# Opening of a fused attention and two feed-forward blocks on one core: a constant's operation that loads the exp table, weight loads and narrowings set behind the first head pairs, and more zero products on TensorE

## The chip, the core and the metric

The kernel runs on one core of one Trainium2 chip. The metric is device time in microseconds (us), the median of the runs. Engine names are those of the profile: PE is TensorE (PEld its weight loads), DVE VectorE, ACT ScalarE, POOL GpSimd, SP SyncE, whose queue issues every DMA here.

## The reference, cut to what matters

Causal attention (2 batches, 12 heads, 448 rows, head size 64) feeds two feed-forward blocks in a row.

```python
scores = scale * np.matmul(q, k.transpose(0, 1, 3, 2))
scores = np.where(np.triu(np.ones((seq, seq), bool), k=1), -1e9, scores)
attn = np.exp(scores - scores.max(-1, keepdims=True))
x = attn / (attn.sum(-1, keepdims=True) + 1e-9) @ v      # 896 tokens x 768
h = x @ w_in                                             # 768 -> 2048
x = np.where(h >= 1, h, np.where(h <= -1, 0, (h + 1) ** 2 / 4)) @ w_out
g = x @ w_gate; out = (g * sigmoid(g) * (x @ w_val)) @ moe2_w_out
```

## The kernel before

**Attention.** The work goes by pairs of heads. Rows 0 to 223 of each batch are token group 0: twelve pairs, one step each, here steps 0 to 11. Rows 224 to 447 are group 1: again twelve pairs, two steps each (336 and 448 key columns), steps 12 to 35. A step is a chain: `scores` on PE (L245, then the mask added by a product with `mask_b`, L251), `greatest` on DVE (row maxima L263, scaled and negated L265), `exps` on ACT (L277), `normalize` on DVE (L288, L289, L301), `turn` on PE (transposes, L312), `turned` on ACT (copy out, L321), `values` on PE (L332, L345), `x_hi` on ACT and `x_lo` on DVE (L352, L356). The tile `s` has two buffers, so the scores of step k+1 wait until the exps of step k-1 have been read out.

**Weights.** Every weight tile (128 x 768, 64-bit words) goes through four DVE or POOL operations and one on ACT (`Weights.operations`): L106, L111 and L115 narrow it to 32 bits, L123 (ACT) and L124 split it into `wh` and `wl`. The first nine tiles are prepared on DVE while the attention runs, a few operations a step (`W.tick`, `TICKS`). The load of a tile is issued from SP; `wraw` has two buffers.

**Products that fill.** From step 14 on, products of the first feed-forward block (`filler`, L68 to L70, here fill products) stand between the attention's PE work. Before that, `zeros` issues products of a zeroed tile (128x512 bf16, L366) into the bank `warm`: 18 (`WARM`) at the start and `HOLD` of them in each of steps 0 to 13. `warm` and the first fill product use the same PSUM buffer, so that product comes after the last zero product.

**Order.** The program's order above is only a priority: a list scheduler in the framework settles the order of each engine's queue when the kernel is built, from its own estimate of when an operand is ready. Each engine then runs its queue strictly in that order. The zero products depend on nothing and go wherever the scheduler sees PE free. `tc.keep_in_program_order(x)` holds `x` at its written place in its engine's queue.

Of the kernel before, what the change touches and what calls it, by code (L numbers as in the profile page):

```python
# [8 lines left out]
F32 = mybir.dt.float32  # L9
# [3 lines left out]
AF = mybir.ActivationFunctionType  # L13
# [14 lines left out]
HALF = DM // 2  # L28
WB = 768
WARM = 18  # L30
HOLD = 1
AHEAD = 3
LASTB = 2
WBUFS = 4
# [13 lines left out]
TURN1 = "A"  # L48
NORM0 = "V"
NORM1 = "V"  # L50
TICKS = (1, 0, 3)


@with_exitstack
def fused_kernel(ctx: ExitStack, tc: tile.TileContext, qk, v, w_in, w_out, w_gv, w_o2, out):
    nc = tc.nc

    const = ctx.enter_context(tc.tile_pool(name="const", bufs=1))
    ident = const.tile([128, 128], F32, name="ident")
    ident_b = const.tile([128, C], BF16, name="ident_b")  # L60
    mask_b = const.tile([128, C], BF16, name="mask_b")
    half_b = const.tile([128, 1], F32, name="half_b")
    xy = ctx.enter_context(tc.tile_pool(name="xy", bufs=2))
    wp = ctx.enter_context(tc.tile_pool(name="wp", bufs=WBUFS))
    ev = ctx.enter_context(tc.tile_pool(name="ev", bufs=2))
# [11 lines left out]
    class Weights:  # L77
# [8 lines left out]
        def load(self, upto):  # L86
            while self.loaded < min(upto, len(self.srcs)):
                src, n = self.srcs[self.loaded]
                t = wp.tile([128, WB], I64, tag="raw", name="wraw", bufs=2)
                nc.sync.dma_start(out=t[:, :n], in_=src)  # L90
                self.raw[self.loaded] = t
                self.loaded += 1
# [5 lines left out]
        def operations(self):  # L98
            for i, (_, n) in enumerate(self.srcs):
                self.load(i + 1)  # L100
                raw = self.raw.pop(i)
                w = raw[:, :n].bitcast(I32).rearrange("p (n t) -> p n t", t=2)
                wt = wp.tile([128, WB], I32, tag="wt", name="wt", bufs=2)
                t = wt[:, :n]

                nc.vector.tensor_scalar(  # L106
                    out=t, in0=w[:, :, 1], scalar1=3, scalar2=0x3FFFFFF8,
                    op0=ALU.logical_shift_left, op1=ALU.bitwise_and,
                )
                yield  # L110
                nc.vector.scalar_tensor_tensor(  # L111
                    out=t, in0=w[:, :, 1], scalar=-0x40000000, in1=t, op0=ALU.bitwise_and, op1=ALU.bitwise_or,
                )
                yield
                nc.vector.scalar_tensor_tensor(  # L115
                    out=t, in0=w[:, :, 0], scalar=29, in1=t, op0=ALU.logical_shift_right, op1=ALU.bitwise_or,
                )
                self.load(i + 3)
                yield
                home = self.stay if WBUFS <= i < EARLY else wp  # L120
                wh = home.tile([128, WB], F32R, tag="wh", name="wh")
                wl = home.tile([128, WB], F32R, tag="wl", name="wl")
                nc.scalar.copy(out=wh[:, :n], in_=t.bitcast(F32))  # L123
                (nc.vector if i < LOW_V else nc.gpsimd).tensor_tensor(  # L124
                    out=wl[:, :n], in0=t.bitcast(F32), in1=wh[:, :n].bitcast(F32), op=ALU.subtract,
                )
                self.got[i] = wh, wl
                self.ready = i + 1
                yield
# [29 lines left out]
    W = Weights(srcs, stay.enter_context(tc.tile_pool(name="stay", bufs=STAY, side="right")))  # L159
# [52 lines left out]
    with ExitStack() as ph:  # L212
# [22 lines left out]
        def scores(k):  # L235

            u, j = steps[k]
            qk_t, _ = ld[u]
            s = ps_s.tile([128, 2, 512], F32, tag="s", name="s")
            k0 = GT if j == 0 else 0  # L240

            for i, (off, w, q0) in enumerate(reversed(SEGS[j])):
                for h in range(2):
                    hd = slice(h * D, (h + 1) * D)
                    nc.tensor.matmul(  # L245
                        out=s[:C, h, off:off + w], lhsT=qk_t[hd, q0:q0 + C], rhs=qk_t[hd, k0:k0 + w],
                        start=(i == 0), stop=False, skip_group_check=True,
                    )
            for off, w, _ in SEGS[j]:
                for h in range(2):  # L250
                    nc.tensor.matmul(  # L251
                        out=s[:C, h, off + w - C:off + w], lhsT=ident_b[:C, :], rhs=mask_b[:C, :],
                        start=False, stop=True, skip_group_check=True,
                    )
            st[k] = {"s": s}
# [27 lines left out]
        def normalize(k):  # L283
# [6 lines left out]
            for i, (off, w, _) in enumerate(segs):  # L290
# [5 lines left out]
                else:  # L296
                    norms = NORM0 if j == 0 else NORM1
                    for h in range(2):
# [6 lines left out]
        def turn(k):  # L305
            u, j = steps[k]
            p = st[k]["p"]
            t = ps_t.tile([128, 2, 512], F32, tag="t", name="t")
            for h in range(2):
                for i in range(NK[j]):  # L310
                    sl = slice(i * C, (i + 1) * C)
                    nc.tensor.transpose(t[:C, h, sl], p[:, h, sl], ident[:C, :C])  # L312
            st[k]["t"] = t

        def turned(k):
            u, j = steps[k]
            if j != 3:
                pts[u] = pp.tile([C, 2, 784], F32, tag="pt", name="pt", bufs=2)
            off, w = (336 if j == 3 else 0), NK[j] * C
            turns = TURN0 if j == 0 else TURN1  # L320
            (nc.vector.tensor_copy if turns[k % len(turns)] == "V" else nc.scalar.copy)(  # L321
                out=pts[u][:, :, off:off + w], in_=st[k].pop("t")[:C, :, :w])
# [41 lines left out]
        def zeros(n):  # L364
            for _ in range(n):
                nc.tensor.matmul(out=warm, lhsT=idle[:, :128], rhs=idle, start=True, stop=True)  # L366
# [2 lines left out]
        make_identity(nc, ident)  # L369
        nc.vector.memset(mask_b, 0.0)  # L370
        nc.vector.memset(half_b, 0.5)
        nc.gpsimd.affine_select(
            out=mask_b[:C, :], in_=mask_b[:C, :], compare_op=ALU.is_ge, fill=MASK,
            base=0, pattern=[[-1, C]], channel_multiplier=1,
        )
        nc.vector.tensor_copy(out=ident_b, in_=ident[:, :C])
        W.load(2)

        fill, done, fresh = None, 0, []

        def filler():
# [16 lines left out]
        for k in range(-1, last + 2):  # L398
            lead, lag = k + 1 < last, k - 2 >= 0
            pv = lag and steps[k - 2][1] != 2  # L400
            kind = 0 if k < first1 else 2 + (k - first1) % 2
            for op in ORDER[kind]:
                if op == "copy" and lag:
                    turned(k - 2)
                elif op == "scores" and lead:
                    scores(k + 1)
                elif op == "max" and lead:
                    greatest(k + 1)
                elif op == "exp" and lead:
                    exps(k + 1)  # L410
                elif op == "norm" and 0 <= k < last:
                    normalize(k)
                elif op == "turn" and 0 <= k - 1 < last:
                    assert "t" not in st.get(k - 2, ())
                    turn(k - 1)
                elif op == "values" and pv:
                    assert not fresh_o and not half_o and "t" not in st[k - 2]
                    fresh_o.append(values(k - 2))
                elif op == "x_hi" and fresh_o:
                    half_o.append(x_hi(*fresh_o.pop()))  # L420
                elif op == "x_lo" and half_o:
                    x_lo(*half_o.pop())
                elif op == "fill" and k >= 0:
                    if k >= first1 + 2:
                        filler()
                    else:
                        zeros(HOLD)
                elif op == "relu" and fresh:
                    half.append(h_relu(*fresh.pop()))
                elif op == "square" and half:  # L430
                    whole.append(h_max(*half.pop()))
                elif op == "g_hi" and whole:
                    split_h.append(g_hi(*whole.pop()))
                elif op == "g_lo" and split_h:
                    g_lo(*split_h.pop())
                elif op == "weights" and k >= 2:
                    W.tick(TICKS[k % 3])
            if lead and steps[k + 1][1] != 3:
                load(steps[k + 1][0] + AHEAD)
        while done < EARLY or fresh or half or whole or split_h:  # L440
            if fresh:
                half.append(h_relu(*fresh.pop()))
            if half:
                whole.append(h_max(*half.pop()))
            if whole:
                split_h.append(g_hi(*whole.pop()))
            if split_h:
                g_lo(*split_h.pop())
            if done < EARLY:
                filler()  # L450
                W.tick()
# [144 lines left out]
```

## Time and profile before

| | us |
|---|---|
| median of 3 runs (lowest, highest) | 628.79 (628.43, 628.95) |
| profiled execution, its own time | 629.75 |
| span in the profile, first to last instruction | 628.0 |
| PE busy in it | 614.7 |
| DVE busy | 361.4 |
| ACT busy | 210.1 |

The span is 1.75 us shorter than that execution's time. PE is busy for nearly all of it, so time can only go where PE idles, where it runs at the lower of its two clocks, or where it does work that isn't needed. The records of neighbouring operations on one engine overlap a little; costs are therefore read from start to start.

### The profile page before, as it was taken

Reading aid. Unit: us, or ns where it says so; the run is one execution under the profiler, and the core shown is the slowest. Engines: PE = TensorE matmul, PEld = TensorE weight load, DVE = VectorE, ACT = ScalarE, POOL = GpSimd, SP = SyncE. Lnnn points to the kernel's source line nnn. Section 1 sums busy time; section 2 is a strip of 40 time slices with the busy share of each in tenths; the row PEclk is TensorE's granted clock in tenths of the full one; section 3 lists DMA queues with packets and bytes.
Section 4 is the critical chain, followed back from the end, with each engine's and each line's share of the span. In section 5 each row is a group of like instructions: output and inputs, shape, how many; then the busy total and the mean of one; then the engine's idle time right before and its main releaser. Section 6 shows DMA issues by size and latency. Waiting matters only on the chain.

```text
span 628.0 us, 8597 instructions
## 1 busy us (share of the span) xinstructions
PE 614.7 (98%) x3367; PEld 537.6 (86%) x3368; DVE 361.4 (58%) x687; ACT 210.1 (33%) x454; POOL 118.1 (19%) x68
## 2 busy tenths in 40 slices
PE   7999999998999999999999999999999999999997
PEld 3676566666999999999999999999999999999997
DVE  3779999865496767534344356556655555532401
ACT  1568766665344433211212132222222222111100
POOL 0000000000221222222323223332222222321300
PEclk9579999999999999999999999999999999999999
DMA  7446544300032232333334333333333333335002
GB/s 245 155 138 212 192 139 163 120 2 2 1 110 91 83 102 85 110 108 110 125 94 137 106 100 102 101 110 129 113 101 108 124 122 100 101 101 177 13 1 88
DMA packets 18664, 67.79 MB, mean 108 GB/s; under 512 B 2112, under 2 KB 6784, under 8 KB 18624
## 3 DMA queue, kind: packets, MB, share of 16 engines
q1 hardware_dynamic: 18624, 67.25, 33.8%
q8 instruction: 26, 0.43, 0.3%
q14 instruction: 14, 0.11, 0.1%
HBM read 64.49 MB, written 2.75 MB: 107 GB/s over the span
## 4 chain that ended last, share of the span: by engine, by line
PE 91%; DVE 5%; ACT 2%; DMA 1%; issue 0%; SPq 0%; ACTq 0%
PE mm L68 22%; PE mm L69 21%; PE mm L70 21%; PE mm L538 5%; PE mm L537 5%; PE mm L536 5%; PE s L245 4%; PE t L312 3%; PE o L345 2%; ACT p L277 1%; PE o L332 1%; PE s L251 1%; DMA wraw<-w_in 1%; DVE s L263 1%; DVE p L301 1%; DVE q L187 0%
## 5 line engine op out<-in xcount | busy, mean ns | idle before, releaser
L124 POOL TENSOR_TENSOR wl<-wt,wh 128x768 fp32r<-128x768 f32 (+1 forms) x61 | 117.2, 1922 | 479.4 <-ACT wh L123 479.4
L123 ACT CAST wh<-wt 128x768 fp32r<-128x768 f32 (+1 forms) x70 | 57.1, 820 | 177.6 <-PE mm L69 107.2
L106 DVE TENSOR_SCALAR wt<-wraw 128x768 int32<-128x768 int32 (+1 forms) x70 | 41.5, 593 | 118.1 <-POOL wl L124 109.2
L70 PE MATMUL mm<-yh,wl 128*128 128x448 f32 x288 | 105.2, 365 | 0.0
L69 PE MATMUL mm<-yl,wh 128*128 128x448 f32 x288 | 105.2, 365 | 0.0
L68 PE MATMUL mm<-yh,wh 128*128 128x448 f32 x288 | 105.2, 365 | 0.0
L68 PE MATMUL mm<-xh,wh 128*128 128x448 f32 x192 | 73.0, 380 | 2.2 <-DVE q L188 2.1
L69 PE MATMUL mm<-xl,wh 128*128 128x448 f32 x192 | 70.7, 368 | 0.0
L70 PE MATMUL mm<-xh,wl 128*128 128x448 f32 x192 | 70.3, 367 | 0.0
L68 PE MATMUL mm<-gh,wh 128*128 128x448 f32 x192 | 70.1, 365 | 0.0
L69 PE MATMUL mm<-gl,wh 128*128 128x448 f32 x192 | 70.1, 365 | 0.0
L70 PE MATMUL mm<-gh,wl 128*128 128x448 f32 x192 | 70.1, 365 | 0.0
L111 DVE SCALAR_TENSOR_TENSOR wt<-wraw,wt 128x768 int32<-128x768 int32 (+1 forms) x70 | 67.5, 964 | 1.4
L115 DVE SCALAR_TENSOR_TENSOR wt<-wraw,wt 128x768 int32<-128x768 int32 (+1 forms) x70 | 65.1, 930 | 1.6
L69 PEld LDWEIGHTS mm<-yl,wh 128*128 128x128 f32 x288 | 54.1, 188 | 4.3
L68 PEld LDWEIGHTS mm<-yh,wh 128*128 128x128 f32 x288 | 54.1, 188 | 4.3
L70 PEld LDWEIGHTS mm<-yh,wl 128*128 128x128 f32 x288 | 54.1, 188 | 4.3
L538 PE MATMUL mm<-wh,ul 128*128 128x384 f32 x168 | 56.1, 334 | 0.0
L536 PE MATMUL mm<-wh,uh 128*128 128x384 f32 x168 | 56.1, 334 | 0.0
L537 PE MATMUL mm<-wl,uh 128*128 128x384 f32 x168 | 56.1, 334 | 0.0
L277 ACT ACTIVATE p<-s,mx 112x112 f32<-112x112 f32 (+3 forms) x96 | 46.5, 499 | 12.8 <-DVE mx L265 9.8
L245 PE MATMUL s<-qk_t 64*112 64x224 f32 (+3 forms) x192 | 39.3, 471 | 4.5 <-ACT p L277 4.5
(62 smaller groups left out, 824.3 us busy)
## 6 DMA issues: line engine op xcount, KB each, us to landing
wraw<-w_gv SPq DMA_DIRECT2D x24, 768.0 KB, 4.2
wraw<-w_in SPq DMA_DIRECT2D x16, 768.0 KB, 4.4
wraw<-w_out SPq DMA_DIRECT2D x12, 768.0 KB, 4.3
wraw<-w_o SPq DMA_DIRECT2D x12, 768.0 KB, 4.2
qk_t<-qk SPq DMA_DIRECT2D x12, 336.0 KB, 3.0
wraw<-w_out SPq DMA_DIRECT2D x6, 512.0 KB, 3.8
qk_t<-qk SPq DMA_DIRECT2D x12, 224.0 KB, 3.3
v_t<-v SPq DMA_DIRECT2D x12, 224.0 KB, 2.8
```

Of the source, the lines that this page charges most:

```text
L68: nc.tensor.matmul(out=ps, lhsT=wh, rhs=xh, start=first, stop=False)
L69: nc.tensor.matmul(out=ps, lhsT=wh, rhs=xl, start=False, stop=False)
L70: nc.tensor.matmul(out=ps, lhsT=wl, rhs=xh, start=False, stop=last)
L111: nc.vector.scalar_tensor_tensor(out=t, in0=w[:, :, 1], scalar=-0x40000000, in1=t, op0=ALU.bitwise_and, op1=ALU.bitwise_or,)
L115: nc.vector.scalar_tensor_tensor(out=t, in0=w[:, :, 0], scalar=29, in1=t, op0=ALU.logical_shift_right, op1=ALU.bitwise_or,)
L123: nc.scalar.copy(out=wh[:, :n], in_=t.bitcast(F32))
L124: (nc.vector if i < LOW_V else nc.gpsimd).tensor_tensor(out=wl[:, :n], in0=t.bitcast(F32), in1=wh[:, :n].bitcast(F32), op=ALU.subtract,)
L245: nc.tensor.matmul(out=s[:C, h, off:off + w], lhsT=qk_t[hd, q0:q0 + C], rhs=qk_t[hd, k0:k0 + w], start=(i == 0), stop=False, skip_group_ch ...
L277: nc.scalar.activation(out=p[:, h, off:off + w], in_=s[:C, h, off:off + w], func=AF.Exp, bias=mx[:, i, h:h + 1], scale=0.125, accum_out=sm ...
L536: nc.tensor.matmul(out=ps, lhsT=c, rhs=a, start=(f == 0), stop=False)
L537: nc.tensor.matmul(out=ps, lhsT=c, rhs=b, start=False, stop=False)
L538: nc.tensor.matmul(out=ps, lhsT=d, rhs=a, start=False, stop=(f == FC2 - 1))
```

## The change

Four edits, all at the opening of the attention. A one-column activation with exp on the constant `half_b` stands ahead of the first real exp. `W.load(2)` moves from ahead of the steps to the end of step 0. The first narrowing of weight tiles 0 and 1 keeps its written place. `HOLD` becomes 12, 6, 4 in steps 0 to 2 and 2 in steps 3 to 13: 44 zero products there in place of 14.

```diff
-HOLD = 1
+HOLD = (12, 6, 4, 2)
+PINNED = 2
+    half_x = const.tile([128, 1], F32, name="half_x")
...
-                nc.vector.tensor_scalar(
+                first = nc.vector.tensor_scalar(
                     out=t, in0=w[:, :, 1], scalar1=3, scalar2=0x3FFFFFF8,
                     op0=ALU.logical_shift_left, op1=ALU.bitwise_and,
                 )
+                if i < PINNED:
+                    tc.keep_in_program_order(first)
...
         nc.vector.memset(half_b, 0.5)
+
+        nc.scalar.activation(out=half_x, in_=half_b, func=AF.Exp)
...
         nc.vector.tensor_copy(out=ident_b, in_=ident[:, :C])
-        W.load(2)
-
...
-                        zeros(HOLD)
+                        zeros(HOLD[min(k, len(HOLD) - 1)])
...
                 load(steps[k + 1][0] + AHEAD)
+            if k == 0:
+                W.load(2)
```

The queues as built show what moves. Lines of the changed kernel are 2 higher from L62 on and 4 higher from L110 to L370 (L106 is L108 there, L111 is L115, L263 is L267, L366 is L370).

DVE, from the constants on, before:

```order
L376 CAST ident_b<-ident 128x112
L106 TENSOR_SCALAR wt<-wraw 128x768
L263 TENSOR_REDUCE s<-s 112x2
L111 SCALAR_TENSOR_TENSOR wt<-wraw,wt 128x768
L263 TENSOR_REDUCE s<-s 112x2 x2
L265 TENSOR_SCALAR mx<-s 112x4
L263 TENSOR_REDUCE s<-s 112x2
L115 SCALAR_TENSOR_TENSOR wt<-wraw,wt 128x768
L265 TENSOR_SCALAR mx<-s 112x4
```

DVE, the same place in the changed kernel:

```order
L382 CAST ident_b<-ident 128x112
L267 TENSOR_REDUCE s<-s 112x2 x3
L269 TENSOR_SCALAR mx<-s 112x4
L267 TENSOR_REDUCE s<-s 112x2
L269 TENSOR_SCALAR mx<-s 112x4
L292 TENSOR_SCALAR sm<-sm 112x4
L293 RECIPROCAL sm<-sm 112x4
L305 TENSOR_SCALAR p<-p,sm 112x112 x2
L305 TENSOR_SCALAR p<-p,sm 112x224 x2
```

The weight operations have left the place between the first maxima; the first of them (L108) now comes behind the scaling of the maxima of step 3.

PE, behind the mask products of step 4, before:

```order
L332 MATMUL o<-pt,v_t 64x224 x2
L332 MATMUL o<-pt,v_t 64x112 x2
L312 MATMUL t<-ident,p 112x112
L245 MATMUL s<-qk_t 112x224
L312 MATMUL t<-ident,p 112x112 x5
L245 MATMUL s<-qk_t 112x224
L245 MATMUL s<-qk_t 112x112 x2
```

PE, the same place in the changed kernel, from the last of two zero products on:

```order
L370 LDWEIGHTS idle
L370 MATMUL mm<-idle 128x512
L249 MATMUL s<-qk_t 112x224
L316 MATMUL t<-ident,p 112x112 x4
L336 MATMUL o<-pt,v_t 64x224 x2
L336 MATMUL o<-pt,v_t 64x112 x2
L316 MATMUL t<-ident,p 112x112 x2
L249 MATMUL s<-qk_t 112x224
L249 MATMUL s<-qk_t 112x112 x2
```

Zero products now stand inside the steps; before, all 14 stood in one run behind the scores of step 1 and 12 are left there. The first fill product has moved from behind `values` of step 2 to behind `values` of step 7.

SP, the first loads, before:

```order
L228 DMA qk_t<-qk 128x448
L229 DMA v_t<-v 112x256
L90 DMA wraw<-w_in 128x768 x2
L228 DMA qk_t<-qk 128x448
L229 DMA v_t<-v 112x256
```

SP in the changed kernel, from the fourth pair's loads on:

```order
L232 DMA qk_t<-qk 128x448
L233 DMA v_t<-v 112x256 x2
L92 DMA wraw<-w_in 128x768
L232 DMA qk_t<-qk 128x448
L92 DMA wraw<-w_in 128x768
L232 DMA qk_t<-qk 128x448
```

The first weight tile now goes out behind the loads of pair 3, the second behind the `qk_t` of pair 4, whose buffer the scores of step 0 must have released.

## Rows read from the trace of the kernel before

**Rows 1.** The page, part 2: PE's granted clock in 40 slices, in tenths.

```profile
PEclk9579999999999999999999999999999999999999
```

**Rows 2.** Busy us (instructions) by stretch: PE, PEld, DVE, ACT, POOL, then granted clock, DMA.

```profile
12.49:15.97 3.48, 0.00 (x1) 0.01 (x1) 3.39 (x9) 2.98 (x10) 0.00 (x0) 0.83 0.70 179
15.97:38.30 22.33, 21.64 (x107) 15.28 (x107) 14.28 (x47) 11.68 (x42) 0.00 (x0) 0.50 0.37 123
40.70:76.24 35.54, 33.89 (x273) 22.39 (x272) 34.43 (x114) 29.71 (x95) 0.00 (x0) 1.00 0.65 208
76.24:117.50 41.26, 40.80 (x274) 27.77 (x272) 40.49 (x99) 27.73 (x69) 0.00 (x0) 1.00 0.54 171
```

**Rows 3.** Timeline of the opening: start, us, engine, line, operation [idle before <- releaser].

```profile
7.96 0.41 PE L251 MATMUL s<-mask_b,ident_b 112*112 112x112 bf16 x4
...
9.30 3.19 PE L366 MATMUL mm<-idle 128*128 128x512 bf16 x13
...
10.27 0.56 DVE L106 TENSOR_SCALAR wt<-wraw 128x768 int32<-128x768 int32 x1 [8.66 <-DMA wraw<-w_in]
...
12.75 0.15 DVE L265 TENSOR_SCALAR mx<-s 112x4 f32<-112x4 f32 x1
...
12.98 1.28 ACT L277 ACT_TABLE_LOAD   x1 [12.98 <-DVE mx L265]
...
14.27 0.35 ACT L277 ACTIVATE p<-s,mx 112x112 f32<-112x112 f32 x1
...
15.79 0.37 ACT L277 ACTIVATE p<-s,mx 112x112 f32<-112x112 f32 x1
...
15.97 1.47 PE L245 MATMUL s<-qk_t 64*112 64x224 f32 x8 [3.48 <-ACT p L277]
```

**Rows 4.** Timeline of PE at granted clock 0.5, steps 5 and 6.

```profile
31.30 1.46 PE L245 MATMUL s<-qk_t 64*112 64x224 f32 x6
32.69 0.62 PE L251 MATMUL s<-mask_b,ident_b 112*112 112x112 bf16 x4
33.24 1.39 PE L332 MATMUL o<-pt,v_t 112*64 112x224 f32 x8
...
35.84 1.32 PE L312 MATMUL t<-ident,p 112*112 112x112 f32 x6
37.10 1.46 PE L245 MATMUL s<-qk_t 64*112 64x224 f32 x8
```

**Rows 5.** Timeline of PE at granted clock 1.0, step 7, steps 11 and 18.

```profile
40.70 0.83 PE L245 MATMUL s<-qk_t 64*112 64x224 f32 x8
...
52.84 0.79 PE L312 MATMUL t<-ident,p 112*112 112x112 f32 x6
53.55 0.83 PE L245 MATMUL s<-qk_t 64*112 64x224 f32 x8
54.31 0.41 PE L251 MATMUL s<-mask_b,ident_b 112*112 112x112 bf16 x4
...
54.91 0.79 PE L332 MATMUL o<-pt,v_t 112*64 112x224 f32 x8
55.64 0.31 PE L312 MATMUL t<-ident,p 112*112 112x112 f32 x1
...
76.24 0.47 PE L68 MATMUL mm<-xh,wh 128*128 128x448 f32 x1
```

**Rows 6.** DVE alone in steps 7 to 11: busy us (instructions), clock, DMA.

```profile
40.70:56.77 16.07, 15.93 (x59) 1.00 0.77 249
```

**Rows 7.** Timeline of DVE there, two weight operations, each with what follows it.

```profile
50.63 0.95 DVE L124 TENSOR_TENSOR wl<-wt,wh 128x768 fp32r<-128x768 f32 x1
51.50 0.15 DVE L265 TENSOR_SCALAR mx<-s 112x4 f32<-112x4 f32 x1
...
53.09 0.55 DVE L106 TENSOR_SCALAR wt<-wraw 128x768 int32<-128x768 int32 x1
53.56 0.62 DVE L263 TENSOR_REDUCE s<-s 112x2 f32<-112x448 f32 x1
```

## The prediction

> **What bounds the kernel now.** I read the clock by slices first. PE is granted full speed (2.4 GHz) everywhere but in the first three slices, 9, 5 and 7 tenths [rows 1], so I cut the attention into stretches [rows 2]. Three things are to be seen. From 12.49 to 15.97 PE does nothing. From 15.97 to 38.30 it is busy by its records, at granted clock 0.50, which is the 1.2 GHz level. From 40.70 on it runs at 1.00 with DVE busy 34.43 of 35.54 us and then 40.49 of 41.26: both engines are full there, and further on PE alone is.
>
> The timeline of the opening says why PE stood still [rows 3]. The mask products of step 0 are through at 8.4, so DVE could take the first maxima then. But its first instruction is the narrowing L106, which waits for a weight tile until 10.27. The maxima are scaled at 12.75, ACT then loads its table (1.28 us), exps run from 14.27, and the scores of step 2, which need the buffer that exps of step 0 read, start at 15.97 after 3.48 us of idle. In that idle time the granted clock fell to half.
>
> What half clock costs is read from start to start. At 0.50: scores 1.39, mask 0.55, values 1.32, transposes 1.26 [rows 4], 4.52 us a step. At 1.00: scores 0.76, mask some 0.3, values 0.73, transposes 0.71 [rows 5], 2.5 us a step. Steps as they happened: step 2 at 15.97 to step 7 at 40.70 is 24.7 us, 4.95 a step; step 7 at 40.70 to step 11 at 53.55 is 12.85 us, 3.21 a step [rows 3, 5]. That later pace is DVE's: 15.93 us busy of 16.07 [rows 6], of which seven weight operations take 4.7 (0.87 a wide one, 0.47 the narrowing, start to start, the last cut off by the stretch's end [rows 7]). The other 11.3 us are five steps, 2.25 each.
>
> **The change, part by part.** *Narrowings.* No weight operation is left on DVE before the maxima of step 3, so the maxima of step 0 start at 8.4. They take no more than 1.2 (half of a step's 2.25): exps can start at 9.6 in place of 14.27. Four exps are 1.52 us [rows 3], so those of step 0 are read out at 11.2 and those of step 1 at 12.8.
>
> *Table load.* It now stands behind a constant written before the first zero product, and ACT has nothing to do until 9.6. Its 1.28 us are hidden by that. Without the new operation the first exps would end at 12.5.
>
> *Zero products, the first 12.* The run of 14 took 9.30 to 12.49 [rows 3], 0.22 each. Twelve end at 11.9, later than the exps at 11.2, so they set the start of step 2's scores: 12.0. That is **4.0 us earlier** than 15.97. PE has no idle stretch there at all.
>
> *Clock.* Nothing in the new order leaves PE idle for long: scores of step 2 at 12.0 to 13.1, six zero products to 14.4, transposes of step 0 (their p is normalised at about 12.4), scores of step 3, four zero products to about 17, and values, whose copy on ACT is out at about 17. I find waits of at most 1 us at steps 4 and 5, behind DVE's first weight tile. In the trace the clock fell after some 2.3 us without any product (a mean of 0.83 over 3.48 us of idle is 1.0 for two thirds of it, then 0.5 [rows 2]), and it held at 1.00 through steps 7 to 11, where the pace leaves PE 0.7 us without work in each 3.21. I take it that it holds. The Trainium skill, TensorE: Matmul & The Clock Gate, section A second HAM failure mode: psum-queue depth-cycling, speaks against this: short idles between groups of matmuls are said to make the clock swing between its levels. The trace differs from step 7 on, where such idles left the clock at 1.00; by that rule the sum would be the slower rival below.
>
> *Steps 2 to 6.* PE's work at full clock between the scores of steps 2 and 7 is five scores with masks (5.3), five turns (3.6), four values (2.9) and 16 zero products (3.4): 15.2 us, so step 7's scores can't start before 27.2. DVE has by the maxima of step 7 seven steps (15.8) and nine weight operations, two tiles of 3.1 and two narrowings (7.1 in all), from 8.4 on, and about 3 us in which it waits for exps (until 16.3 it has 5 us of work in 8): 34.3, where before they ended at 45.7. That is 11.4 earlier. The pace 3.21 with some 0.2 for the zero products gives the same, 12.0 + 5 x 3.4 = 29.0 for the scores, 11.7 earlier than 40.70. I take **11.2**; the ends are 9.7 and 13.5 (PE's floor).
>
> *Steps 7 to 18.* From 76.24 on, the first run of six fill products inside values, PE's queue is the same row by row to the end. Up to there the new queue has 16 more zero products (3.4 us) and three more fill products (18 against 15, 0.6), and DVE has two more weight operations (11 against 9, 1.7). Least: DVE's 1.7 less the 1.1 that it idles there [rows 2], 0.6. Most: all 4.0 on PE's path. PE has some 5 us of slack in these 35.5 (30.2 us of work by the same counts), but the two queues are strict and hold one another up, so I take **2.4 given back**.
>
> *Behind 76.24.* DVE comes there with 20 weight operations done where it had 23, and catches up by step 29, past the place (step 26, about 114 us) where its queue went slack before. One more operation falls into the full stretch, two into slack. Given back: 0 to 1.7, **0.8** taken.
>
> *Loads.* SP sends the first weight tile behind the loads of pair 3, before that at 3.52, now at about 4.5 to 8. Before it was ready 6.8 us after its issue with all else in flight; so it is there by 11 to 15, and DVE asks for it at about 17.7. Cost nothing; if it came after 17.7, each us of delay would stand ahead of the normalisation of step 2.
>
> Sum: -11.2 + 2.4 + 0.8 = -8.0. Against the profiled execution's own 629.75 that is 621.75. The median of the runs stands 0.96 below that execution, so I say **620.8**.
>
> **The rivals.** *The zero products land on the path* (0.15). PE and DVE are both full from step 7 on, so every zero product may delay the chain: -9.7 + 4.0 + 1.7 = -4.0, 624.8. For it: DVE's share in rows 2. Against it: PE's 0.7 us of slack a step.
>
> *The clock falls all the same* (0.06), the slower side. If the pairs of matmuls, waits and zero products don't hold it, steps 2 to 6 run at 4.52 and 3.2 zero products at twice 0.22 each, 5.9 us a step; step 7 starts at 12.0 + 29.5 = 41.5, 0.8 later than before, and with 2.4 and 0.8 on top the time is 632.8. It decides from the third slow step on: each costs 5.9 - 3.4 = 2.5, and three of them eat 7.5 of the 8.0. For it: at half clock the steps 2 to 6 of before did not raise it for 22 us. Against it: nothing like the 3.48 us of idle is left, and steps 7 to 11 held it.
>
> *The opening was hidden anyway* (0.03). If DVE's total work to 76.24 set the time, an earlier start would not count, and it would be 628.8. Against it: DVE idles 8 of 22.33 us in the slow stretch [rows 2].
>
> *Nothing is given back* (0.06): the zero products all fall into PE's slack, and step 7 comes at the pace of 3.4 a step: -11.7 + 0.6 = -11.1, 617.7.
>
> **How the numbers follow.** 0.70 goes to the forecast, whose own range is 618.5 to 622.3 (step 7 earlier by 13.5 or by 9.7, 3.2 given back). 617 to 625 takes in the case without loss and the one with the zero products on the path, and leaves out the slow clock, no change, and tails: some 0.15. A difference under 0.2% (1.3 us) can't be told from none here. Faster by more: 0.70 + 0.15 + 0.06 = 0.91; within: 0.03; slower: 0.06.
>
> **What would show it.** In the changed profile the table load stands before 4 us and the first exp at about 9.7. The granted clock is 1.0 from the opening on, and its row loses the 5 and the 7. Scores of step 2 start at about 12, of step 7 at 28 to 31, and the run of six inside values at 66 to 70 where it was 76.24. Fill products start later. From there every piece is earlier by the same amount, within 1 us. I am wrong if the clock's row shows a 5 behind 12 us, if DVE's first L108 waits for its DMA, or if PE shows idle time behind zero products that DVE could have used.

## The result, and the profile after

The changed kernel takes 623.37 us (median of 4 runs, 622.67 to 624.03) beside 628.87 (4 runs, 628.43 to 630.1) of the kernel before: a ratio of 0.9909 [0.9891, 0.9927]. It is faster by 5.5 us, where 8.0 were forecast. Its profiled execution took 624.03, span 622.2.

The page: busy time of PE and its granted clock in 40 slices.

```profile
PE 612.5 (98%) x3394; PEld 534.1 (86%) x3398; DVE 362.6 (58%) x687; ACT 210.4 (34%) x455; POOL 118.0 (19%) x68
...
PEclk9999999999999999999999999999999999999999
```

The 5 and the 7 of [rows 1] are gone: no slice at half clock is left. The stretches from the scores of step 2 to those of step 7, from there to the first run of six fill products, and on from it (columns as in [rows 2]):

```profile
13.14:29.88 16.74, 15.99 (x138) 10.79 (x139) 14.64 (x51) 12.16 (x48) 0.00 (x0) 1.00 0.54 162
29.88:70.20 40.32, 39.75 (x291) 24.79 (x292) 38.12 (x118) 30.82 (x98) 0.00 (x0) 1.00 0.61 198
70.20:111.50 41.30, 40.38 (x270) 27.65 (x270) 39.56 (x95) 27.00 (x65) 0.00 (x0) 1.00 0.47 141
```

Steps 2 to 6 take 16.74 us where they took 24.73. The second stretch takes 40.32 where it took 35.54 [rows 2]: 4.8 are given back there, and PE and DVE are both nearly full in it (39.75 and 38.12 us busy). A second profile of the same kernel has 16.73 and 40.32. From the run of six on (70.20, before 76.24) the gain is 6.0, and 5.8 at the span's end.

The timeline of the opening (PE, DVE and ACT; columns as in [rows 3]):

```profile
0.73 1.28 ACT L377 ACT_TABLE_LOAD   x1 [0.73 <-PEq L592]
...
1.19 6.86 PE L370 MATMUL mm<-idle 128*128 128x512 bf16 x18 [1.19 <-DVE half_b L375]
7.98 1.20 PE L249 MATMUL s<-qk_t 64*112 64x224 f32 x10
...
9.56 1.49 DVE L267 TENSOR_REDUCE s<-s 112x2 f32<-112x224 f32 x3 [7.95 <-PE s L255]
...
10.46 2.75 PE L370 MATMUL mm<-idle 128*128 128x512 bf16 x11
...
11.22 0.35 ACT L281 ACTIVATE p<-s,mx 112x112 f32<-112x112 f32 x1 [8.99 <-DVE mx L269]
...
13.14 0.83 PE L249 MATMUL s<-qk_t 64*112 64x224 f32 x8
...
14.15 1.46 PE L370 MATMUL mm<-idle 128*128 128x512 bf16 x6
...
17.13 1.03 PE L370 MATMUL mm<-idle 128*128 128x512 bf16 x4
18.85 0.79 PE L336 MATMUL o<-pt,v_t 112*64 112x224 f32 x8 [0.70 <-ACT pt L325]
```

PE no longer stands still before the scores of step 2: the zero products end at 13.1 and the scores follow at 13.14, after exps from 11.22. The opening itself is late, and how late differs between executions: the scores of step 0 begin at 7.98, where the profile of before has them at 6.83, since the 18 zero products at the start took 6.86 us. A second profile of the same changed kernel has 7.14, and in those of the variants below the start lies between 6.78 and 8.03. Stage times are therefore compared counted from the scores of step 0 where that matters.

The timeline around steps 7 to 9, where the largest loss begins (DVE and PE):

```profile
29.88 0.83 PE L249 MATMUL s<-qk_t 64*112 64x224 f32 x8
...
30.41 0.55 DVE L108 TENSOR_SCALAR wt<-wraw 128x768 int32<-128x768 int32 x1
...
30.96 0.53 DVE L108 TENSOR_SCALAR wt<-wraw 128x768 int32<-128x768 int32 x1
31.40 0.95 DVE L115 SCALAR_TENSOR_TENSOR wt<-wraw,wt 128x768 int32<-128x768 int32 x1
...
32.46 0.96 DVE L119 SCALAR_TENSOR_TENSOR wt<-wraw,wt 128x768 int32<-128x768 int32 x1
...
34.31 0.96 DVE L128 TENSOR_TENSOR wl<-wt,wh 128x768 fp32r<-128x768 f32 x1
...
34.86 1.89 PE L370 MATMUL mm<-idle 128*128 128x512 bf16 x8
...
36.09 0.15 DVE L269 TENSOR_SCALAR mx<-s 112x4 f32<-112x4 f32 x1
...
36.68 0.79 PE L336 MATMUL o<-pt,v_t 112*64 112x224 f32 x8
...
38.74 0.83 PE L249 MATMUL s<-qk_t 64*112 64x224 f32 x8
...
70.20 0.47 PE L70 MATMUL mm<-xh,wh 128*128 128x448 f32 x1
```

Five weight operations stand on DVE between the scores of step 7 (29.88) and the scaling of their maxima (36.09), and PE meanwhile runs eight zero products in a row. In the kernel before there were three between the scores (40.70) and that scaling:

```profile
40.73 0.94 DVE L124 TENSOR_TENSOR wl<-wt,wh 128x768 fp32r<-128x768 f32 x1
...
42.12 0.53 DVE L106 TENSOR_SCALAR wt<-wraw 128x768 int32<-128x768 int32 x1
...
44.72 0.92 DVE L111 SCALAR_TENSOR_TENSOR wt<-wraw,wt 128x768 int32<-128x768 int32 x1
45.56 0.15 DVE L265 TENSOR_SCALAR mx<-s 112x4 f32<-112x4 f32 x1
```

### The profile page after: what moved, and what is told of

Same layout as the page of the kernel before. It is cut to its first block, busy times and chain, and to the rows that moved or that the text cites. A ratio compares the mean times of both kernels' runs of the same rounds, so it can differ in the third digit from the quotient of the medians.

```text
span 622.2 us, 8660 instructions
## 1 busy us (share of the span) xinstructions
PE 612.5 (98%) x3394; PEld 534.1 (86%) x3398; DVE 362.6 (58%) x687; ACT 210.4 (34%) x455; POOL 118.0 (19%) x68
## 4 chain that ended last, share of the span: by engine, by line
PE 90%; DVE 5%; ACT 4%; issue 1%; ACTq 0%
PE mm L70 22%; PE mm L71 21%; PE mm L72 21%; PE mm L542 5%; PE mm L544 5%; PE mm L543 5%; PE s L249 3%; PE t L316 3%; ACT p L281 2%; PE mm L370 2%; PE o L349 2%; PE o L336 1%; DVE s L267 1%; DVE p L305 1%; PE s L255 1%
## 5 line engine op out<-in xcount | busy, mean ns | idle before, releaser
L108 DVE TENSOR_SCALAR wt<-wraw 128x768 int32<-128x768 int32 (+1 forms) x70 | 41.5, 593 | 108.9 <-POOL wl L128 108.8
L115 DVE SCALAR_TENSOR_TENSOR wt<-wraw,wt 128x768 int32<-128x768 int32 (+1 forms) x70 | 67.6, 966 | 1.3
L70 PEld LDWEIGHTS mm<-xh,wh 128*128 128x128 f32 x192 | 36.1, 188 | 6.9 <-DVE q L192 3.5
```

The lines of the kernel that those rows point to most:

```text
L70: nc.tensor.matmul(out=ps, lhsT=wh, rhs=xh, start=first, stop=False)
L108: first = nc.vector.tensor_scalar(out=t, in0=w[:, :, 1], scalar1=3, scalar2=0x3FFFFFF8, op0=ALU.logical_shift_left, op1=ALU.bitwise_and,)
L115: nc.vector.scalar_tensor_tensor(out=t, in0=w[:, :, 1], scalar=-0x40000000, in1=t, op0=ALU.bitwise_and, op1=ALU.bitwise_or,)
```

## Experiments

All were timed beside the kernel before on the same chip; ratios are to it. "Clock" is the mean granted clock of one run. The experiments stand here by topic and not in the order in which they ran, so that an expectation can speak of a result further down.

**One part alone: loads and narrowings.** From the changed kernel, without the constant's operation and with the zero products of before.

```diff
-HOLD = (12, 6, 4, 2)
+HOLD = (1,)
...
-        nc.scalar.activation(out=half_x, in_=half_b, func=AF.Exp)
```

> The kernel before with only the loads moved and the first narrowings held in place; no table operation, HOLD 1. The maxima of step 0 start about 2 us earlier, the exps still wait for the table load. Account after the first runs: PE idles less than 1 us behind the 14 zero products, the clock holds, and the time is that of the kernel without added zero products, 620 to 621.5. Rival: each of the early 1.3 us of the table counts, 621.3 to 622.5, or the clock falls, 627 to 629.

Measured: 624.0 us, 0.9914 [0.9897, 0.9931]: the whole gain of the change. But the clock was 0.995 to 0.996 in all six runs. The timeline of its PE:

```profile
34.29 0.79 PE L336 MATMUL o<-pt,v_t 112*64 112x224 f32 x8 [1.57 <-ACT pt L325]
35.02 1.32 PE L316 MATMUL t<-ident,p 112*112 112x112 f32 x6
36.27 1.46 PE L249 MATMUL s<-qk_t 64*112 64x224 f32 x8
```

and the granted clock of the same kernel in two stretches there:

```profile
35.00:36.00 1.00, 1.00 (x8) 0.81 (x6) 1.00 (x4) 1.00 (x6) 0.00 (x0) 0.74 0.78 310
36.00:37.00 1.00, 1.00 (x6) 0.68 (x6) 1.00 (x5) 0.74 (x2) 0.00 (x0) 0.50 0.72 227
```

After 1.57 us of waiting before the values of step 5 the clock falls to 0.5, and it is back to 1.0 only after 42; the opening itself held it, and so did a wait of 1.26 us before the values of step 2 (23.44). So this part removes the stall of the opening, and one later wait costs part of the gain.

**One part alone: zero products.**

```diff
-HOLD = 1
+HOLD = (12, 6, 4, 2)
...
-                        zeros(HOLD)
+                        zeros(HOLD[min(k, len(HOLD) - 1)])
```

> The kernel before with only HOLD changed: 21 zero products stand behind the scores of step 1 where 14 did, others inside the steps. Table load and weight work stay in front. If it is the idle stretch behind these products alone that makes the clock fall, it shrinks from 3.5 to about 2 us, and runs will be found with and without a fall: 622 to 631, mean clock 0.98 to 1.0. If the zero products in the steps raise the clock again quickly after a fall, 624 to 626 throughout. If the early exps are what counts, 630 or more.

Measured: 626.13 us, 0.9951 [0.9931, 0.997], over twelve runs. Seven runs at a clock of 0.994 to 0.997 took 626.1 to 627.8. Of the five at 0.999 to 1.0, four took 622.8 to 625.8 and one, the profiled one, 630.53. That one did not lose its time in the opening: from the first product that reads `gh` to the end it takes 388.71 us, where the thirteen other traces all have 382.94 to 382.98, at a granted clock of 1.00. Why is open. Zero products alone hold the clock in part of the runs, and give somewhat over half of the gain.

**One part alone: the table load.**

```diff
+    half_x = const.tile([128, 1], F32, name="half_x")
...
+        nc.scalar.activation(out=half_x, in_=half_b, func=AF.Exp)
```

> The kernel before with only the constant's exp added: exps of step 0 end 1.3 us earlier, PE's idle stretch behind the 14 zero products shrinks from 3.5 to about 2.2 us. If the clock falls as before: 627.5 (1.3 less). If 2.2 us is short enough to keep it: 619 to 621, since nothing is added to PE's work. Runs of both kinds are possible, told apart by their mean clock.

Measured: 629.02 us, 0.9993 [0.9978, 1.0009], over twelve runs: no change, at a clock of 0.980 to 0.988 in all of them. The profiled execution, 626.33, is the fastest of the twelve, and its weight tile landed early: the first narrowing starts at 8.78, where the profile of before has 10.27. Its first DVE instruction, its PE before the scores of step 3, and the granted clock in two stretches:

```profile
8.78 0.56 DVE L107 TENSOR_SCALAR wt<-wraw 128x768 int32<-128x768 int32 x1 [7.17 <-DMA wraw<-w_in]
...
15.69 0.63 PE L246 MATMUL s<-qk_t 64*112 64x224 f32 x2 [1.03 <-ACT p L278]
```

```profile
16.00:17.00 1.00, 1.00 (x5) 0.40 (x3) 1.00 (x5) 0.00 (x0) 0.00 (x0) 0.98 0.95 359
17.00:18.00 1.00, 1.00 (x6) 0.82 (x5) 1.00 (x2) 0.00 (x0) 0.00 (x0) 0.50 0.17 61
```

PE's longest wait in the opening is 1.03 us here, not 3.48, and the clock falls all the same, at 17; it stays at 0.5 until 34. How long PE waited in the eleven slower runs no profile shows. Hiding the table load alone did not keep the clock in any run, and bought nothing in the median.

**One part undone: the added zero products** (14 in steps 0 to 13, as before).

```diff
-HOLD = (12, 6, 4, 2)
+HOLD = (1,)
```

> All edits but the added zero products (HOLD back to 1; 14 stay behind the scores of step 1 and a few places behind). My account: the early exps alone keep PE from idling as long as the 2.3 us after which the clock fell before, so the granted clock stays at 1.0 and the 30 zero products that are gone give back 2 to 4 us: 619.5 to 621.5. Rival: the zero products are what holds the clock; it falls at the steps 2 or 3, five steps run at the slow pace, and the time is 628 to 632.

Measured: 620.03 us, 0.9859 [0.9842, 0.9877]. On another chip, beside a repeat of the changed kernel:

> The kernel with all edits but the added zero products once more, for its spread: 619.8 to 620.2 where the clock holds, 622 to 623 where it falls for some 4 to 6 us behind the values of step 5. If the first look was luck, most runs are of the second kind, as they were for the kernel with only the narrowings moved.

> The changed kernel once more, beside the kernel without its added zero products on one chip: 622.5 to 624 with clock 0.999 to 1.0.

Measured: 620.42 us, 0.986 [0.9838, 0.9882], against 623.52, 0.9911 [0.989, 0.9931] for the changed kernel. The two intervals don't meet: the 30 added zero products cost 3.1 us net. The clock was 0.999 to 1.0 in eight of the nine runs of this version; the ninth, at 0.997, took 622.46. Timeline of its PE (first set of runs):

```profile
12.16 0.83 PE L249 MATMUL s<-qk_t 64*112 64x224 f32 x8
...
15.03 0.79 PE L336 MATMUL o<-pt,v_t 112*64 112x224 f32 x8
...
27.04 0.83 PE L249 MATMUL s<-qk_t 64*112 64x224 f32 x8
...
33.43 0.79 PE L336 MATMUL o<-pt,v_t 112*64 112x224 f32 x8 [1.57 <-ACT pt L325]
...
66.11 0.47 PE L70 MATMUL mm<-xh,wh 128*128 128x448 f32 x1
```

and its stretch from the scores of step 7 to the run of six:

```profile
27.04:66.11 39.07, 36.58 (x275) 22.82 (x274) 37.78 (x118) 30.66 (x98) 0.00 (x0) 1.00 0.64 204
```

Two things are to be seen. The values of step 0 start 7.8 us after the scores of step 0 (7.22), where the changed kernel needs 10.9. There the six zero products stand ahead of transposes that could run (they start at 15.45, without the added ones at 13.17), and ACT copies these out only behind the exps of step 2, at 18.07, where it did so ahead of them, at 14.04. And the stretch from step 7 on takes 39.07 us without any added zero product, 3.5 more than before: that part of the loss is not theirs.

**One part undone: loads and narrowings** (the load back at its old place, no narrowing held).

```diff
-PINNED = 2
+PINNED = 0
...
+        W.load(2)
...
-            if k == 0:
-                W.load(2)
```

> The table load and the zero products stay, the two loads and the narrowings go back to where they were. My account: the first maxima wait again for the weight tile until about 10.3, the exps of step 0 end at about 14.4 in place of 12.7, scores of step 2 come 1.5 to 2 us later, the clock holds: 625 to 626. Rival: what is late is only DVE's opening, which the zero products and the full DVE of later steps swallow: 623 to 624. If the clock falls in the wait behind the zero products: above 628.

Measured: 622.92 us, 0.9911 [0.9888, 0.9934]. Four runs at a clock of 1.0 took 622.2 to 623.4; one at 0.997 took 625.62, one at 0.991 took 626.84. With table load and zero products the moved narrowings aren't needed for the gain, but two of six runs lose the clock for a while without them.

Its trace shows why they bring nothing here. Counted from the scores of step 0, those of step 7 come 3.3 us later than in the changed kernel (25.20 against 21.90). But from there to the transposes behind the run of six fill products it takes less (this version, then the changed kernel):

```profile
33.06:72.01 38.95, 38.45 (x299) 25.60 (x300) 38.26 (x123) 30.84 (x99) 0.00 (x0) 1.00 0.61 199
29.88:72.70 42.82, 42.25 (x307) 26.59 (x308) 40.40 (x124) 31.75 (x100) 0.00 (x0) 1.00 0.58 186
```

DVE has 14 weight operations in the first of these stretches and 17 in the second. What is moved out of the opening is done later, where DVE is full.

**One part undone: the table load.**

```diff
-        nc.scalar.activation(out=half_x, in_=half_b, func=AF.Exp)
```

> The changed kernel without the constant's exp: the table load of 1.28 us stands before the first real exp again. My account: exps of step 0 end 1.3 us later, so do the scores of step 2 and all behind: 624.5 to 625. Rival: the start of the scores is set by the zero products in front of them and the loss is swallowed by slack: 623 to 623.8.

Measured: 623.21 us, 0.9902 [0.9889, 0.9914], the same as with it. The scores of step 2 start 6.2 us after those of step 0 in place of 5.2, and 17 zero products fill the place in front of them, with one left behind them where there were six: the exps come 1 us later, and zero products that would have stood further on fill that time. So the rival held.

**How many zero products, and where.** None from step 3 on; then four a step from step 3 on; then none in steps 1 and 2.

```diff
-HOLD = (12, 6, 4, 2)
+HOLD = (12, 6, 4, 0)
```

> HOLD (12, 6, 4, 0): the zero products of steps 3 to 13 (22) are gone, those of steps 0 to 2 stay. If these 22 stand on PE's path, as step 7 to 18 of the changed kernel suggest (40.3 us in place of 35.5), 619 to 621, and fill products start early again. If they stand in PE's slack and cost nothing, 622.5 to 624. If they hold the clock, above 626 with a 5 in the clock's row.

Measured: 624.89 us, 0.9921 [0.9903, 0.9939], clock 0.991 to 0.996 in all six runs: between the second case and the third. PE waits 1.57 us before the values of step 5 (35.86), and the granted clock reads:

```profile
36.00:37.00 1.00, 1.00 (x10) 0.67 (x10) 1.00 (x6) 1.00 (x7) 0.00 (x0) 1.00 1.00 409
37.00:38.00 1.00, 1.00 (x7) 0.79 (x8) 1.00 (x4) 1.00 (x5) 0.00 (x0) 0.73 0.74 263
38.00:39.00 1.00, 1.00 (x9) 0.68 (x7) 1.00 (x5) 0.70 (x3) 0.00 (x0) 0.50 0.53 193
```

The eight zero products that the changed kernel runs at 34.86 cover this wait. With them the clock was 0.999 to 1.0 in all ten runs of the changed kernel, so they are an insurance against this fall.

```diff
-HOLD = (12, 6, 4, 2)
+HOLD = (12, 6, 4, 4)
```

> The changed kernel with 4 zero products in place of 2 in each of steps 3 to 13, 22 more of 0.215 us (4.7 us of PE time). On PE's path: 627.5 to 628.5. In slack: 623 to 624.5. From the kernel without added ones (30 fewer, 3.3 us less) I expect about half on the path: 625.5 to 626.5.

Measured: 622.75 us, 0.9901 [0.9885, 0.9918]: 22 more zero products cost nothing that can be told (the changed kernel has 0.9909 and 0.9911). From the scores of step 0 to those of step 9 it takes 30.4 us, the changed kernel 30.8, and the version without added ones 27.9. So the price isn't one per piece.

```diff
-HOLD = (12, 6, 4, 2)
+HOLD = (12, 0, 0, 2)
```

> HOLD (12, 0, 0, 2): the six and four zero products that stand in front of the first transposes and the first values are gone, those of the later steps stay (fewer in all, as two a step fall into the idle places behind steps 4 and 7). Account from the runs so far: the ten in steps 1 and 2 delay a chain in which each engine waits for the next, 2 to 3 us; later ones fall into PE's slack and keep the clock. So clock 1.0 in every run and 620 to 621. Rival: it is their number that costs, 0.11 us each as between 14 and 44: 622 to 622.5.

Measured: 622.02 us, 0.9884 [0.9861, 0.9906], 1.5 us below the repeat of the changed kernel on the same chip, though the intervals overlap; clock 0.999 to 1.0. From step 0 to step 9 it takes 29.4 us. So about half of the price lies with the ten zero products in steps 1 and 2, as far as one version can tell: some of its later ones stand at other places too (seven before the values of step 2).

**The five weight operations in step 7 spread out**, with no added zero products. `TICKS` sets how many operations DVE takes per step.

```diff
-HOLD = (12, 6, 4, 2)
+HOLD = (1,)
...
-TICKS = (1, 0, 3)
+TICKS = (1, 1, 2)
```

> No added zero products, and the weight operations spread evenly over the steps (TICKS 1, 1, 2 in place of 1, 0, 3). If the wait of 1.57 us at the values of step 5 comes from five weight operations in a row on DVE, it gets shorter, the clock has no reason to fall, and the time is 618.5 to 620 in every run. If the clock falls all the same, or the spread operations lengthen every step, 621 to 624.

Measured: 621.8 us, 0.988 [0.9859, 0.9902], beside 620.42 with the old `TICKS`: no gain, rather 1.4 us worse. The wait of 1.57 us is gone (the values of step 5, at 32.37, follow the mask products of 31.82), and the clock held in all six runs. But from the scores of step 7 to the run of six DVE has sixteen weight operations as before, and that stretch takes 39.95 us where the second profile of the version with the old `TICKS` has 39.11. That the operations come in a burst isn't what costs.

## Why the prediction was right or wrong

**The clock** was the heart of it, and right. No slice of the changed kernel is at half speed, and the version with the table load alone, where it falls at 17, gains nothing. The table load was rightly called hidden in the kernel as changed: without it, 623.21.

**Scores of step 2.** Forecast 12.0, found 13.14. 1.15 of that is the later start (7.98 against 6.83). Counted from the scores of step 0, the zero products came as forecast; the first exp came 0.5 later than the 9.6 forecast, since the maxima took 1.66 us and not at most 1.2 (9.56 to 11.22), and the zero products covered that.

**Steps 2 to 6.** Forecast: scores of step 7 at 29.5, 11.2 earlier. Found: 29.88, 10.8 earlier. The size was right by luck, since errors of both signs met in it. The start was 1.15 late, and zero products cost 0.37 a step, not 0.2 (without the added ones the same five steps take 14.88 us, with them 16.74). Against that, the pace without them was 2.98 a step and not 3.21.

**Steps 7 to 18: here the forecast failed.** The step "I take 2.4 given back" was mis-sized: 4.8, beyond the 4.0 that it named as most. The groups of weight operations on DVE between the scores of step 7 and the run of six, before (40.70 to 76.24; count, busy us, mean ns of one, idle before them):

```profile
L124 DVE TENSOR_TENSOR wl<-wt,wh 128x768 fp32r<-128x768 f32 x3 | 2.8, 944 | 0.0
L115 DVE SCALAR_TENSOR_TENSOR wt<-wraw,wt 128x768 int32<-128x768 int32 x3 | 2.8, 935 | 0.0
L111 DVE SCALAR_TENSOR_TENSOR wt<-wraw,wt 128x768 int32<-128x768 int32 x3 | 2.8, 934 | 0.0
...
L106 DVE TENSOR_SCALAR wt<-wraw 128x768 int32<-128x768 int32 x3 | 1.6, 546 | 0.0
```

and after (29.88 to 70.20):

```profile
L115 DVE SCALAR_TENSOR_TENSOR wt<-wraw,wt 128x768 int32<-128x768 int32 x4 | 3.8, 953 | 0.0
L119 DVE SCALAR_TENSOR_TENSOR wt<-wraw,wt 128x768 int32<-128x768 int32 x4 | 3.8, 951 | 0.0
L128 DVE TENSOR_TENSOR wl<-wt,wh 128x768 fp32r<-128x768 f32 x4 | 3.8, 951 | 0.5 <-ACT wh L127 0.5
L108 DVE TENSOR_SCALAR wt<-wraw 128x768 int32<-128x768 int32 x4 | 2.2, 541 | 0.0
```

Twelve operations (10.0 us) have become sixteen (13.6): 3.6 us. The prediction counted 9 and 11, which is right from the scaled maxima of step 7 on, but its stretch begins at the scores. Between the two stand the three operations of before and the five of after that are shown above. The prediction had both 11.2 to 11.4 earlier; the scores came 10.8 earlier, their maxima only 9.5 (45.56 to 36.09), and no term held that difference. The version without added zero products agrees: the same sixteen operations, and 3.5 us given back. The other 1.25 of the 4.8 are zero products (40.32 against 39.07). The version with loads and narrowings undone shows it from the other side. From the scores of step 7 to the transposes behind the run of six it has 14 operations, seven zero products and 38.95 us; before had 13 operations, no zero product and 38.06 (40.70 to 78.76); the version without added zero products has 17 operations and 41.57 (27.04 to 68.61). One operation more goes with 0.9 us, four more with 3.5. The version with the spread operations, 16 in 42.46 (26.85 to 69.31), lies off this line, so where they stand counts too; how is open.

**The zero products' price** in one sum, changed kernel against the version without the added ones: 70.20 - 66.11 = 4.09 at the run of six, less 0.76 for the later start, is 3.3; 2.1 of it arises before the scores of step 7 and 1.25 behind them. The rival "the zero products land on the path" (624.8) was thus right in part: the time lies between it and the forecast, and outside the forecast's own range (618.5 to 622.3), but not every zero product delays the chain, as 22 more of them show. The slack of PE, 0.7 us a step, was no cover for pieces that its strict queue runs ahead of ready work. Which of them cost is settled in part only: by the stage times half lies in steps 1 and 2 (30.8 - 29.4 of 30.8 - 27.9), and why 22 more from step 3 on cost nothing is open.

**Behind the run of six** 0.2 were given back, not 0.8. The run itself started at 70.20, just outside the 66 to 70 that was named as a sign. **The loads** cost nothing: the first L108 (19.52) did not wait for its DMA.

**The rival of a falling clock** did not come true in the changed kernel, but it was nearer than its 0.06 said: in two variants (loads and narrowings alone; no zero products from step 3 on) no run kept a mean clock above 0.996, and in the profiled run of each it fell at step 5. The waits of at most 1 us that the prediction found at steps 4 and 5 are 1.57 us where no zero products fill them. The prediction's reading, some 2.3 us without products before a fall, was too simple, since it fell after waits of 1.03 and 1.57 us, and yet held in eight of the nine runs of the version whose two profiles both show the same wait of 1.57 us. What decides that is open; no run here separates it. The falls after short waits are of the kind that the Trainium skill, TensorE: Matmul & The Clock Gate, section A second HAM failure mode: psum-queue depth-cycling, reports of another kernel, whose clock swung with short idles between groups of matmuls. The changed kernel's own trace, at 1.00 in all three stretches above with a wait of 0.70 us (18.85), does not show it.

## What to carry to other kernels

Filler products that hold the clock are worth having only where PE would wait: put ahead of ready work in a strict queue, 30 of them cost 3.1 us, so remove the stall first, then add as few as the granted clock needs. Time each part alone and each part undone: here the moved loads and narrowings alone gave the whole gain (624.0), yet without them the other two parts gave it too (622.9), the table load alone gave none, and the best version was the change without its added zero products (620.0 and 620.4). Work that is moved off a stalled opening isn't gone; look for where it is done instead. When a stage's start moves, count the queue's work from the same point on every engine; scores and maxima of one step were 6.2 us apart, and two operations fell in between.

## What the hardware showed that was not expected

The zero products at the start run at half pace, 0.43 us each, for a while in which the profile's granted clock reads 1.00, and how long differs between executions: the 18 took 5.71 us in the profile of before, 6.86 and 6.03 in two of the changed kernel. That moves everything behind them by up to 1.2 us.

The granted clock fell after waits as short as 1.03 us and, once down, stayed at 0.5 for some 7 us (loads and narrowings alone), 17 us (table load alone) and over 22 us (the kernel before). PE's records are nearly gapless in that time (14.31 of 15.00 us between 18 and 33 with the table load alone). The time follows it from run to run of one kernel: in one set of runs of the kernel before, those at a mean clock of 0.988 took 626.4 and 626.5 us, at 0.984 around 629.1, at 0.981 around 630.1; one run at 0.984 took 635.7 and is an exception.
